# Causal mask by a matmul behind the scores, score banks in twos, casts moved to POOL, loads with third buffers

## The chip, the cores and the metric

The kernel runs on one core of a Trainium2 chip. The core has five engines that run side by side, each through its own list of instructions in order: TensorE (PE; its weight loads are shown apart as PEld), VectorE (DVE), ScalarE (ACT), GpSimd (POOL) and SyncE (SP), which here only issues transfers. TensorE writes to PSUM, eight banks of 128 partitions x 512 float32 words. The metric is the time of one execution on the device in microseconds (us). TensorE's clock has two levels, 1.2 and 2.4 GHz; the profile gives what was granted as a share of the higher one.

## The reference

Attention over 4 batches x 8 heads, 576 positions, head size 64, then two feed-forward blocks. The change touches attention alone.

```python
def _attn_ref(q, k, v, s):
    scores = scale * np.matmul(q, k.transpose(0, 1, 3, 2))
    causal = np.triu(np.ones((S, S), dtype=bool), k=1)
    cum = np.cumsum(np.maximum(s, 0.0), axis=-1)
    bias = -(cum[:, :, :, None] - cum[:, :, None, :])
    scores = np.where(causal, -1000000000.0, scores + np.minimum(bias, 0.0))
    scores = scores - np.max(scores, axis=-1, keepdims=True)
    attn = np.exp(scores)
    attn = attn / (np.sum(attn, axis=-1, keepdims=True) + 1e-09)
    return np.matmul(attn, v)
# then, on x = attention's output as 2304 rows of 512:
#   h = max(x @ w1, x @ w2, x @ w3);  x2 = h @ w_out
#   each row of x2 goes to one of 8 experts:  gate * (relu(x2 @ w1[e]) @ w2[e])
```

Because the bias of a row is the same but for a constant that the softmax removes, a key's bias alone (a running sum of s, times 8) is added to the scores. Everything above the diagonal must vanish after the exponential.

## The kernel before, in words

**A step is one pair of heads**; there are 16 (PORD gives their order). The two heads' q and k lie in the upper and lower 64 partitions. For precision each of q and k is split (split, L199 to 212) into a rounded part, made by a copy on ScalarE (L208), and the rest, made by a subtraction on POOL (L209), both in the tile hl; a score is the sum of three products of such parts.

**Scores** (L217 to 266). The 576 queries are cut into five chunks (QC), and a chunk sees only the keys up to its own end: 576, 448, 320, 192 and 64 of them. The 576 are done in two halves of 288. A chunk or half is a group of six matmuls of 64 rows (L247), three for each head, the heads in turn, into one bank per head from a pool of three (ps_s). VectorE then does one instruction per head (L253): score plus bias into SBUF (tile e), with the running minimum as a side result, since the sign is turned. ScalarE takes the exponential and its row sum (L261).

**The mask** is part of the bias. POOL adds a triangle of -8e9 to the last 128 columns of the key bias bt before it is used (L232), again for the next chunk once VectorE has used the one before (L257), and into a copy bs for the two smallest chunks (L233, L234).

**Behind the scores** each step's e is transposed on PE, 28 blocks of 128x128 into banks of a pool of three (ps_t, L292), copied out by VectorE and ScalarE in turn (L295, L297), and multiplied by v (L318, L321). The reciprocal of the row sums (L271, L272) goes through PE and a round trip to DRAM to become the factor rb, with which VectorE scales the result (L322). This runs a step or so behind the scores.

**Two side jobs** run in the same time. Weights of the first feed-forward block arrive as 64-bit numbers and are converted (convert, L112 to 129): request on SP, then ScalarE (L119), VectorE (L120 to 122), a DMA from POOL (L124) and POOL (L127). From the sixth step on, PE also does a part of that block's projections in the gaps ("fill", L140 to 144).

**What sets the order.** A scheduler orders each engine's instructions by priorities and by its own model of times when the program is built; issue_after ties one instruction behind another, high_priority draws it forward. The kernel asks for loads two steps ahead (L_AHEAD); whether a load can start is decided by its buffers: two for q and k (QR_BUFS), four of bt, two steps' worth (B_BUFS), two for raw weights (RAW_BUFS). SP issues in order, so that a load that waits for its buffer holds those behind it. After attention come the rest of the first block, the routing and the experts, which the change leaves alone.

## Time and profile before

| | |
|---|---|
| Median of 3 runs | 831.02 us (830.81 to 872.44) |
| The profiled execution | 835.91 us, span 834.1 us |
| Busy share of the span | PE 91%, PEld 77%, DVE 61%, ACT 45%, POOL 51% |
| Mean granted clock of TensorE | 0.956 |
| DMA over the span | 129 GB/s |

The span runs from the first to the last instruction of the profiled execution. Busy shares are means over stages of different kinds: attention ends at about 313 us, and what a change there is worth has to be read from that part. In a row of the trace, "out<-in" names the tiles written and read, and an engine's idle time is put down to what it waited for last.

### The profile page before, as it was taken

What the parts mean: (1) busy time and instruction counts of PE and PEld (TensorE: products, weight loads), DVE (VectorE), ACT (ScalarE), POOL (GpSimd) and SP (SyncE); (2) the same over time, 40 slices, a digit from 0 to 9 for tenths busy, and PEclk for the clock granted to TensorE, in tenths of its full rate; (3) what the DMA queues carried; (4) which work ended last, traced back from release to release, by engine and by line L of the source; (5) the groups of instructions that cost most, each with busy time, mean ns of one, the idle gap of its engine ahead of it and who ended that gap; (6) DMA issues with size and microseconds to landing.
All of it is one profiled execution on the core that took longest, in us unless ns stands there. A gap on an engine that the chain in (4) does not pass through costs nothing.

```text
span 834.1 us, 14064 instructions
## 1 busy us (share of the span) xinstructions
PE 759.9 (91%) x4778; PEld 645.0 (77%) x4778; DVE 511.1 (61%) x1382; ACT 376.9 (45%) x924; POOL 425.2 (51%) x484
## 2 busy tenths in 40 slices
PE   2958899979999999989999999999799799999993
PEld 1635566757777878969999989998688699999882
DVE  6556564656554556878466879466464667667720
ACT  2646555545555544442222232165354555656621
POOL 6566565454534402572324363386345767766730
PEclk9988799969999999999999999999899999999998
DMA  7455644436432114421110211375643757656610
GB/s 203 140 147 161 179 132 122 132 119 189 147 101 95 46 39 163 149 94 44 10 49 11 58 46 27 86 265 168 118 157 139 253 191 254 238 195 237 205 48 17
DMA packets 43265, 107.89 MB, mean 129 GB/s; under 512 B 9200, under 2 KB 13168, under 8 KB 43184
## 3 DMA queue, kind: packets, MB, share of 16 engines
q1 hardware_dynamic: 38128, 94.79, 36.4%
q0 software_dynamic: 4912, 11.82, 4.5%
q8 instruction: 39, 0.64, 0.4%
q14 instruction: 42, 0.34, 0.1%
q10 hardware_dynamic: 144, 0.29, 0.1%
HBM read 92.95 MB, written 12.10 MB: 126 GB/s over the span
## 4 chain that ended last, share of the span: by engine, by line
PE 52%; DMA 16%; DVE 13%; POOL 7%; issue 6%; ACT 2%; SPq 1%; POOLq 0%; DVEq 0%; ACTq 0%
PE a_ps L140 5%; PE t_ps L292 5%; PE a_ps L143 5%; PE a_ps L144 4%; PE s_ps L247 4%; DMA w_raw<-in_w 4%; PE o_ps L318 4%; DMA e_raw<-in_we 3%; PE h_ps L650 3%; PE h_ps L653 3%; PE h_ps L654 3%; PE y_ps L681 3%; PE y_ps L682 3%; DMA table<-meta,si 3%; PE y_ps L683 3%
## 5 line engine op out<-in xcount | busy, mean ns | idle before, releaser
L140 PE MATMUL a_ps<-xh,w_h 128*128 128x384 f32 (+2 forms) x492 | 161.1, 328 | 1.7 <-DVE h L346 1.3
L143 PE MATMUL a_ps<-xl,w_h 128*128 128x384 f32 (+2 forms) x492 | 158.6, 322 | 0.9 <-POOL xl L335 0.9
L144 PE MATMUL a_ps<-xh,w_l 128*128 128x384 f32 (+2 forms) x492 | 157.2, 320 | 0.8 <-POOL w_l L127 0.8
L620 DVE TENSOR_TENSOR e_l<-e_raw,e_h 128x512 fp32r<-128x512 f32 x80 | 111.1, 1402 | 52.5 <-ACT e_h L619 50.6
L620 POOL TENSOR_TENSOR e_l<-e_raw,e_h 128x512 fp32r<-128x512 f32 x80 | 108.9, 1382 | 39.4 <-ACT e_h L619 32.4
L247 PE MATMUL s_ps<-hl 64*128 64x288 f32 (+4 forms) x576 | 86.6, 367 | 34.6 <-DVE mn L253 27.9
L619 ACT CAST e_h<-e_raw 128x512 fp32r<-128x512 f32 x160 | 93.1, 621 | 54.9 <-DMA e_raw<-in_we 45.8
L261 ACT ACTIVATE e<-e,mn 128x576 f32<-128x576 f32 (+2 forms) x144 | 83.6, 582 | 51.4 <-DVE mn L253 51.2
L247 PEld LDWEIGHTS s_ps<-hl 64*128 64x128 f32 x576 | 54.1, 208 | 58.6 <-DVE mn L253 36.7
L140 PEld LDWEIGHTS a_ps<-xh,w_h 128*128 128x128 f32 x492 | 93.2, 190 | 6.0 <-DVE h L346 3.0
L143 PEld LDWEIGHTS a_ps<-xl,w_h 128*128 128x128 f32 x492 | 93.2, 189 | 3.7 <-POOL xl L335 1.4
L144 PEld LDWEIGHTS a_ps<-xh,w_l 128*128 128x128 f32 x492 | 93.1, 189 | 1.5 <-POOL w_l L127 1.0
L507 DVE CUSTOM_DVE_ANT_0 junk<-x,wg 128x512 bf16<-128x512 f32 x96 | 71.4, 743 | 27.9 <-ACT x L581 26.7
L650 PE MATMUL h_ps<-x2t,e_h 128*128 128x256 f32 x288 | 80.5, 284 | 4.4 <-DVE gl L656 4.2
L653 PE MATMUL h_ps<-x2t,e_h 128*128 128x256 f32 x288 | 81.5, 284 | 0.0
L654 PE MATMUL h_ps<-x2t,e_l 128*128 128x256 f32 x288 | 81.3, 283 | 0.0
L568 POOL TENSOR_TENSOR fl<-h,fh 128x384 fp32r<-128x384 f32 x36 | 43.8, 1220 | 71.9 <-ACT fh L567 64.0
L292 PE MATMUL t_ps<-ident,e 128*128 128x128 f32 x448 | 70.8, 303 | 1.2 <-ACT r_t L276 0.8
L681 PE MATMUL y_ps<-e_h,gh 128*128 128x512 f32 x152 | 62.6, 412 | 5.8 <-ACT gh L655 5.4
L292 PEld LDWEIGHTS t_ps<-ident,e 128*128 128x128 f32 x448 | 56.5, 155 | 11.7 <-issue 4.4
L253 DVE CUSTOM_DVE_ANT_0 e<-s_ps,bt 128x288 f32<-128x288 f32 (+2 forms) x96 | 47.1, 519 | 23.5 <-POOL bt L257 12.2
L683 PE MATMUL y_ps<-e_h,gl 128*128 128x512 f32 x152 | 61.3, 403 | 0.0
(180 smaller groups left out, 1535.7 us busy)
## 6 DMA issues: line engine op xcount, KB each, us to landing
e_raw<-in_we SPq DMA_DIRECT2D x80, 512.0 KB
w_raw<-in_w SPq DMA_DIRECT2D x24, 512.0 KB
qk_r<-in_qk SPq DMA_DIRECT2D x15, 576.0 KB
bt<-dk SPq DMA_DIRECT2D x30, 288.0 KB
v_r<-in_vd SPq DMA_DIRECT2D x16, 320.0 KB
rb<-r_d SPq DMA_DIRECT2D x32, 144.0 KB
x2d<-x SPq DMA_DIRECT2D x18, 256.0 KB
w_h<-w_z POOLq DMA_DIRECT2D x9, 256.0 KB, 4.9
```

Source lines behind the costliest of these rows:

```text
L140: ins = P.matmul(a_ps, wh[:, c], xh[:, c], start=c == 0, stop=False).ins
L143: P.matmul(a_ps, wh[:, c], xl[:, c], start=False, stop=False)
L144: P.matmul(a_ps, wl[:, c], xh[:, c], start=False, stop=c == 3)
L247: ins = P.matmul(s_ps[j], flat[js, o:o + 128], hl[js, b, 0, k0:k0 + n], start=i == 0, stop=i == 2).ins
L292: last_t[0] = P.transpose(out=t_ps[:, n * 128:(n + 1) * 128], in_=e[:, EOFF[c] + kb * 128:EOFF[c] + (kb + 1) * 128], identity=ident).ins
L619: A.copy(out=h, in_=raw[:, a])
L620: (G if a else V).tensor_tensor(out=lo, in0=raw[:, a], in1=h.bitcast(F32), op=ALU.subtract)
L650: ins = P.matmul(h_ps, w(hs, f, c), xt[:, 0, c], start=c == 0, stop=False).ins
L653: P.matmul(h_ps, w(hs, f, c), xt[:, 1, c], start=False, stop=False)
L654: P.matmul(h_ps, w(ls, f, c), xt[:, 0, c], start=False, stop=c == 3)
L681: P.matmul(y_ps, u["h"][:, f, cs], hs[f], start=f == 0, stop=False)
L683: P.matmul(y_ps, u["l"][:, f, cs], hs[f], start=False, stop=f == NF2 - 1)
```

## The change

1. **Mask on PE.** Behind the six matmuls of a chunk, two bf16 matmuls (one per head) add the product of a diagonal of -2^33 (neg) and a triangle of ones (tri; tri_2 for the smallest chunk) to the last 128 columns of the scores; VectorE's -0.125 turns that into a large positive number. All additions on POOL go, and bs with them.
2. **Score banks in twos.** ps_s has two buffers of two banks (both heads in one tile) in place of three of one bank; ps_t has two banks in place of three.
3. **Casts on POOL.** The rounded parts of q and k are made by POOL, but for the first step.
4. **Third buffers** for q and k and, by the pair, for the bias.
5. **Raw weights a step ahead.** Their request is issued in the step before the one that converts them.
6. At the start, the identity and the constants come over ScalarE's queue, and VectorE does one of the first step's subtractions.

```diff
@@ -72,6 +72,6 @@
 FILL_N = [0, 9, 8, 6]
-PSB = (3, 3, 1, 1)
+PSB = (2, 2, 1, 1)
 HL_BUFS = 2
-QR_BUFS = 2
-B_BUFS = 4
+QR_BUFS = 3
+B_BUFS = 6
 E_N = 4
@@ -111,5 +111,9 @@
 
-        def convert(f, k, pool, tag, rp_, lo_on=None, early=False):
+        def raw_in(f, k, rp_):
             raw = rp_.tile([128, 512, 2], I32, tag="raw", name="w_raw")
             SP.dma_start(out=raw.rearrange("p n c -> p (n c)"), in_=w64[f, :, k * 512:(k + 1) * 512].bitcast(I32))
+            return raw
+
+        def convert(f, k, pool, tag, rp_, lo_on=None, early=False, raw=None):
+            raw = raw_in(f, k, rp_) if raw is None else raw
             h = pool.tile([128, 512], F32R, tag=tag, name="w_h")
@@ -160,3 +164,5 @@
             ps_f = es.enter_context(tc.tile_pool(name="ps_f", bufs=PSB[3], space=PSUM))
-            mask = ap1.tile([128, 256], F32, name="mask")
+            cst_f = ap1.tile([128, 192], F32, name="cst_f")
+            neg = ap1.tile([128, 128], BF16, name="neg")
+            tri_2 = ap1.tile([128, 64], BF16, name="tri_2")
             xb = [None] * B
@@ -188,4 +194,4 @@
                 if p == 0:
-                    SP.dma_start(out=mask, in_=cst[:, 256:512])
-                    SP.dma_start(out=ident, in_=cst[:, 0:128])
+                    A.dma_start(out=ident, in_=cst[:, 0:128])
+                    A.dma_start(out=cst_f, in_=cst[:, 128:320])
                 return p, x, bts
@@ -201,12 +207,13 @@
                 hl = qkp.tile([128, 2, 2, S], F32R, name="hl", bufs=HL_BUFS)
+                for t in (1, 0):
+                    (G.tensor_copy if p else A.copy)(out=hl[:, 0, t], in_=x[:, t])
                 if p == 0:
-                    for t in (1, 0):
-                        A.copy(out=hl[:, 0, t], in_=x[:, t])
-                    decay(bts[0], cums[:, 0])
+                    G.tensor_scalar(out=neg, in0=ident, scalar1=-2.0 ** 33, scalar2=None, op0=ALU.mult)
+                    G.tensor_copy(out=tri, in_=cst_f[:, 0:128])
+                    G.tensor_copy(out=tri_2, in_=cst_f[:, 128:192])
                 for t in (1, 0):
-                    if p:
-                        A.copy(out=hl[:, 0, t], in_=x[:, t])
-                    ins = G.tensor_tensor(out=hl[:, 1, t], in0=x[:, t], in1=hl.bitcast(F32)[:, 0, t], op=ALU.subtract).ins
+                    ins = (V if p == 0 and t else G).tensor_tensor(out=hl[:, 1, t], in0=x[:, t], in1=hl.bitcast(F32)[:, 0, t], op=ALU.subtract).ins
                 if p == 0:
-                    decay(bts[1], cums[:, 1])
+                    for j in range(2):
+                        decay(bts[j], cums[:, j])
                 return ins, (hl, bts)
@@ -227,10 +234,2 @@
                 sums.append(l)
-                bss = []
-                for j in range(2):
-                    bt = bts[j]
-                    bs = qkp.tile([128, 256], F32, name="bs", bufs=B_BUFS)
-                    G.tensor_tensor(out=bt[:, 448:576], in0=bt[:, 448:576], in1=mask[:, 128:256], op=ALU.add)
-                    G.tensor_tensor(out=bs[:, 64:256], in0=bt[:, 0:192], in1=mask[:, 64:256], op=ALU.add)
-                    G.tensor_tensor(out=bs[:, 0:64], in0=bt[:, 0:64], in1=mask[:, 0:64], op=ALU.add)
-                    bss.append(bs)
                 for c in (4, 3, 2, 1, 0):
@@ -239,3 +238,4 @@
                     for k0, n in [(0, w)] if c < 4 else [(0, 288), (288, 288)]:
-                        s_ps = [ps_s.tile([128, 512], F32, name="s_ps")[:, 0:n] for _ in range(2)]
+                        s_2 = ps_s.tile([128, 2, 512], F32, name="s_ps")
+                        s_ps = [s_2[:, j, 0:n] for j in range(2)]
                         ins = None
@@ -246,3 +246,6 @@
                                 with tc.high_priority() if ins else ExitStack(), tc.issue_after(ins) if ins else ExitStack():
-                                    ins = P.matmul(s_ps[j], flat[js, o:o + 128], hl[js, b, 0, k0:k0 + n], start=i == 0, stop=i == 2).ins
+                                    ins = P.matmul(s_ps[j], flat[js, o:o + 128], hl[js, b, 0, k0:k0 + n], start=i == 0, stop=i == 2 and k0 + n < w).ins
+                        for j in range(2 if k0 + n == w else 0):
+                            with tc.high_priority(), tc.issue_after(ins):
+                                ins = P.matmul(s_ps[j][:, max(n - 128, 0):n], neg, tri_2 if c == 0 and j else tri[:, 0:min(n, 128)], start=False, stop=True).ins
                         for j in range(2):
@@ -251,8 +254,4 @@
                             ec = es_[j][:, EOFF[c] + k0:EOFF[c] + k0 + n] if c else e0[rows]
-                            bias_ = bts[j][:, k0:k0 + n] if c > 1 else bss[j][:, 64:256] if c else bss[j][rows, 0:64]
-                            V.tensor_tensor_reduce(out=ec, in0=s_ps[j][rows], in1=bias_, scale=-0.125, scalar=first[j], op0=ALU.add, op1=ALU.min, accum_out=mn[rows, col:col + 1])
+                            V.tensor_tensor_reduce(out=ec, in0=s_ps[j][rows], in1=bts[j][rows, k0:k0 + n], scale=-0.125, scalar=first[j], op0=ALU.add, op1=ALU.min, accum_out=mn[rows, col:col + 1])
                             first[j] = mn[rows, col:col + 1]
-                            if c > 2 and k0 + n == w:
-                                k1 = QC[c - 1][1] - 128
-                                G.tensor_tensor(out=bts[j][:, k1:k1 + 128], in0=bts[j][:, k1:k1 + 128], in1=mask[:, 128:256], op=ALU.add)
                     for j in range(2 if c else 1):
@@ -424,2 +420,3 @@
             todo = []
+            raws = {}
             n_head = 2
@@ -440,4 +437,7 @@
                 for n in CONV.get(p, ()):
-                    with tc.issue_after(exps[-1 - CONV_LAG]), tc.issue_after(last_load[0]):
-                        convert(n // 3, n % 3, w0p, "w0", rawp, early=True)
+                    with tc.issue_after(exps[-1 - CONV_LAG]):
+                        convert(n // 3, n % 3, w0p, "w0", rawp, early=True, raw=raws.pop(n))
+                for n in CONV.get(p + 1, ()):
+                    with tc.issue_after(last_load[0]):
+                        raws[n] = raw_in(n // 3, n % 3, rawp)
                 if p % (H // 2) == H // 2 - 1:
...
```

The parts left out move the constants' columns in the table cst and their loads after the first step.

The order of PE in the fourth step, before (s_ps are scores, t_ps transposes and r the row sums):

```order
L247 MATMUL s_ps<-hl 128x288 x12
L247 MATMUL s_ps<-hl 128x448 x6
L247 MATMUL s_ps<-hl 128x320
L274 MATMUL t_ps<-ident,r 9x128
L292 MATMUL t_ps<-ident,e_119 128x128 x8
L247 MATMUL s_ps<-hl 128x320 x5
L292 MATMUL t_ps<-ident,e_119 128x128 x2
L247 MATMUL s_ps<-hl 128x192
L292 MATMUL t_ps<-ident,e_119 128x128 x4
L292 MATMUL t_ps<-ident,e_120 128x128 x4
L247 MATMUL s_ps<-hl 128x192 x5
```

and now, in the same step, from its chunk of 448 on:

```order
L247 MATMUL s_ps<-hl 128x448 x6
L250 LDWEIGHTS neg
L250 MATMUL s_ps<-tri,neg 128x128
L250 LDWEIGHTS neg
L250 MATMUL s_ps<-tri,neg 128x128
L320 MATMUL t_ps<-pt,v_r 64x64 x2
L273 MATMUL t_ps<-ident,r 9x128
L247 MATMUL s_ps<-hl 128x320 x6
```

Before, one matmul of a chunk stood apart from the other five, with transposes between; now the six stand together and two mask matmuls behind them, and the transposes come between whole groups.

The order of POOL about the first conversions of weights, before (hl is the split q and k, bt and bs the bias, w_h and w_l converted weights):

```order
L209 TENSOR_TENSOR hl<-qk_r,hl 128x576 x2
L124 DMA w_h<-w_z 128x512
L257 TENSOR_TENSOR bt<-bt,mask 128x128 x4
L127 TENSOR_TENSOR w_l<-w_z,w_h 128x512
L124 DMA w_h<-w_z 128x512
L232 TENSOR_TENSOR bt<-bt,mask 128x128
L127 TENSOR_TENSOR w_l<-w_z,w_h 128x512
L232 TENSOR_TENSOR bt<-bt,mask 128x128
L233 TENSOR_TENSOR bs<-bt,mask 128x192
L234 TENSOR_TENSOR bs<-bt,mask 128x64
```

and now, at the same place:

```order
L209 CAST hl<-qk_r 128x576 x2
L215 TENSOR_TENSOR hl<-qk_r,hl 128x576
L128 DMA w_h<-w_z 128x512
L215 TENSOR_TENSOR hl<-qk_r,hl 128x576
L131 TENSOR_TENSOR w_l<-w_z,w_h 128x512
```

Before, mask additions stood behind weight instructions that wait for a DMA; now casts and subtractions of q and k stand there.

The order of SP about the first raw weights, before (r_d and rb are the sums' round trip):

```order
L277 DMA r_d<-r_t 2x1x64
L279 DMA r_d<-r_t 4x128 x2
L179 DMA qk_r<-in_qk 128x1152
L282 DMA rb<-r_d 64x576 x2
L186 DMA bt<-dk 128x576 x2
L114 DMA w_raw<-in_w 128x1024 x2
L216 DMA v_r<-in_vd 128x640
```

and now:

```order
L185 DMA qk_r<-in_qk 128x1152
L192 DMA bt<-dk 128x576 x2
L114 DMA w_raw<-in_w 128x1024 x2
L276 DMA r_d<-r_t 2x1x64
L278 DMA r_d<-r_t 4x128 x2
L281 DMA rb<-r_d 64x576 x2
```

Before, the raw weights stood behind the second step's round trip; now they stand ahead of the first step's. Each request still stands behind two loads of the bias.

## Rows read from the trace of the kernel before

**Rows 1.** Windows: stretch, length, busy time (count) of PE, PEld, DVE, ACT, POOL; clock, DMA.

```profile
24.30:52.40 28.10, 26.27 (x183) 17.65 (x184) 15.36 (x63) 18.03 (x56) 14.06 (x24) 1.00 0.45 127
52.40:95.70 43.30, 30.69 (x181) 19.77 (x179) 24.22 (x79) 21.24 (x60) 25.20 (x37) 0.73 0.54 168
95.70:172.30 76.60, 71.04 (x511) 53.01 (x509) 45.66 (x144) 41.54 (x119) 41.12 (x60) 0.95 0.45 138
172.30:196.70 24.40, 19.85 (x115) 14.16 (x115) 13.18 (x37) 10.25 (x31) 11.92 (x18) 0.72 0.44 136
196.70:219.60 22.90, 21.52 (x168) 17.23 (x166) 16.71 (x49) 12.39 (x34) 11.26 (x17) 1.00 0.56 166
219.60:312.40 92.80, 92.74 (x715) 73.36 (x714) 48.22 (x173) 48.56 (x145) 37.69 (x60) 1.00 0.25 78
```

**Rows 2.** Timeline of the fourth step: start, duration, engine and instruction, [idle before <-releaser].

```profile
49.35 0.90 SPq L114 DMA_DIRECT2D w_raw<-in_w  x2
...
56.25 0.66 ACT L119 ACTIVATE w_z<-w_raw 128x512 f32<-128x512 f32 x1 [5.01 <-DMA w_raw<-in_w]
...
56.94 0.55 DVE L120 TENSOR_SCALAR w_z<-w_z 128x512 int32<-128x512 int32 x1 [3.46 <-ACT w_z L119]
...
58.77 1.22 PE L247 MATMUL s_ps<-hl 64*128 64x288 f32 x6 [4.83 <-DVE mn L253]
```

**Rows 3.** Timeline of the fifth step.

```profile
75.89 0.45 DVE L120 TENSOR_SCALAR w_z<-w_z 128x512 int32<-128x512 int32 x1 [3.02 <-ACT w_z L119]
...
79.36 1.48 PE L247 MATMUL s_ps<-hl 64*128 64x448 f32 x5 [2.65 <-DVE mn L253]
...
87.08 1.27 POOL L127 TENSOR_TENSOR w_l<-w_z,w_h 128x512 fp32r<-128x512 f32 x1 [4.75 <-DMA w_h<-w_z]
...
88.80 0.49 DVE L253 CUSTOM_DVE_ANT_0 e<-s_ps,bt 128x320 f32<-128x320 f32 x1 [1.85 <-POOL bt L257]
...
89.35 1.13 PE L247 MATMUL s_ps<-hl 64*128 64x64 f32 x6 [1.63 <-DVE mn L253]
```

**Rows 4.** Timeline of the tenth step.

```profile
175.39 3.39 DVE L271 TENSOR_SCALAR r<-l 128x9 f32<-128x9 f32 x1
...
176.01 2.74 POOL L209 TENSOR_TENSOR hl<-qk_r,hl 128x576 fp32r<-128x576 f32 x2
...
179.09 0.38 PE L274 MATMUL t_ps<-ident,r 128*9 128x128 f32 x1 [2.71 <-DVE r L272]
```

**Rows 5.** Waits of 24.3 to 219.6 us: who for whom, us, times, longest.

```profile
DVE e L253 <- POOL bt L257: 9.7, 6, 3.1
...
PE s_ps L247 <- DVE mn L253: 18.2, 13, 4.8
...
ACT w_z L119 <- DMA w_raw<-in_w: 16.9, 8, 5.0
```

**Rows 6.** Timeline of PE in the thirteenth step.

```profile
243.70 0.87 PE L247 MATMUL s_ps<-hl 64*128 64x448 f32 x6
244.50 1.31 PE L292 MATMUL t_ps<-ident,e 128*128 128x128 f32 x10
245.57 0.38 PE L140 MATMUL a_ps<-xh,w_h 128*128 128x288 f32 x1
...
252.57 0.29 PE L247 MATMUL s_ps<-hl 64*128 64x64 f32 x1
252.79 0.40 PE L144 MATMUL a_ps<-xh,w_l 128*128 128x288 f32 x1
```

**Rows 7.** Groups of POOL by form: busy us, mean ns, idle before.

```profile
L209 POOL TENSOR_TENSOR hl<-qk_r,hl 128x576 fp32r<-128x576 f32 x32 | 47.2, 1495 | 2.4 <-ACT hl L204 2.0 <-ACT hl L208 0.3
...
L397 POOL CAST tri<-tri_f 128x128 bf16<-128x128 f32 x1 | 0.3, 287 | 0.0
```

**Rows 8.** Groups of DVE, then one line's instructions with min/median/max ns.

```profile
L271 DVE TENSOR_SCALAR r<-l 128x9 f32<-128x9 f32 x16 | 8.9, 557 | 9.8 <-ACT e L261 9.8
...
L271 DVE TENSOR_SCALAR r<-l x16: 163/175/3390, 26.6 to 313.4; 128x9 f32<-128x9 f32 x16
```

More of the change, by code (lines that the diff above doesn't have):

```diff
@@ L392, in fused_kernel @@
             queue(0, front(0), vv)
-            tri_f = ap1.tile([128, 128], F32, name="tri_f")
-            SP.dma_start(out=tri_f, in_=cst[:, 128:256])
-            G.tensor_copy(out=tri, in_=tri_f)
             G.memset(ones, 1.0)
             G.memset(acc[:, 0, :], 0.0)
-            SP.dma_start(out=off, in_=cst[:, 512:512 + E])
-            SP.dma_start(out=iota, in_=cst[:, 520:584])
+            SP.dma_start(out=off, in_=cst[:, 320:320 + E])
+            SP.dma_start(out=iota, in_=cst[:, 328:392])
             sent = ap1.tile([128, TABLE // 128, 2], F32, name="sent")
@@ L886, in _layout @@
     e2 = i["moe2_w2"].reshape(E, 4, 2, 128, DM).transpose(0, 1, 3, 2, 4).reshape(E, 4, 128, 1024)
-    cst = np.zeros((128, 584), np.float32)
+    cst = np.zeros((128, 392), np.float32)
     cst[:, 0:128] = np.eye(128)
     cst[:, 128:256] = np.triu(np.ones((128, 128)), 1)
-    cst[:, 384:512] = np.triu(np.full((128, 128), -8.0e9), 1)
-    cst[:, 256:320] = np.tile(cst[0:64, 384:448], (2, 1))
-    cst[:, 512:520] = np.arange(E) * STRIDE
-    cst[:, 520:584] = np.arange(64)
+    cst[:, 256:320] = np.tile(np.triu(np.ones((64, 64)), 1), (2, 1))
+    cst[:, 320:328] = np.arange(E) * STRIDE
+    cst[:, 328:392] = np.arange(64)
     csi = (np.arange(NT)[None, :] * 128 + np.arange(128)[:, None]).astype(np.int32)
```

## The prediction, made before the changed kernel was run

> **What bounds the kernel now.** I read the table of windows first, then the timeline inside the worst windows, then the waits, and last the pitch of TensorE's instructions.
>
> The windows [rows 1] cut attention at the starts of its 16 steps (a step is one pair of heads). From 24.30 us (second step) to 312.40 us it takes 288.1 us. In the last 92.80 us of that PE is busy 92.74 us at clock 1.00: it is the bound there, and nothing that another engine saves shows. Before that it loses time in two ways: it idles, and after idling its granted clock falls to the lower level, 1.2 GHz, so that its work takes twice as long. A window's idle time is its length less PE's busy time; its loss to the clock is its length times (1 - PEclk). In the order of the rows: 1.8 + 0; 12.6 + 11.7; 5.6 + 3.8; 4.6 + 6.8; 1.4 + 0; 0.1 + 0. That is 26.0 idle and 22.3 by the clock, 48.3 us in all, and half of it, 24.3 us, lies in the fourth and fifth steps, 52.40 to 95.70. The last 520 us, after attention, are touched by no part of the change.
>
> Why PE idles there is seen in the timelines. In the fourth step [rows 2] the raw weights are asked for at 49.35 and are used by ScalarE only at 56.25, after 5.01 us of waiting; VectorE stands behind that with its in-order conversion (3.46 us), and the matmul of the scores behind VectorE (4.83 us). In the fifth [rows 3] there are two spells: PE waits 2.65 us for VectorE, which did late raw weights first (3.02 us of waiting for them), and then a mask addition comes late from POOL, in whose order (w_h, w_l) instructions that wait for a DMA stand ahead of it: VectorE waits 1.85 us for the masked bias, and PE 1.63 us for VectorE. In the tenth step [rows 4] the small TENSOR_SCALAR of the row sums takes 3.39 us while POOL works through two subtractions, and PE waits 2.71 us for it. The waits of 24.3 to 219.6 us [rows 5] give the sums: VectorE waits 9.7 us for the masked bias, ScalarE 16.9 us for raw weights, PE 18.2 us for VectorE's reductions of the scores.
>
> **The change, part by part.** The sum is made against the profiled execution, 835.9 us; it stands 4.9 us (0.6%) over the median of the runs, 831.0, and the result is shifted by that.
>
> *Waits that lose their cause.* With third buffers the bias for the step after next no longer waits for this step's scores; raw weights are asked for a step ahead of their conversion, and a step is some 14 us where it is short (two take 28.10 us [rows 1]) against the 6.9 us from request to use in [rows 2]; and VectorE needs nothing of POOL any more for its bias. So the causes in the fourth and fifth steps go. I take 20 of the 24.3 us in 52.40 to 95.70, 7 of 11.4 in 172.30 to 196.70 (what held VectorE there were mask additions and two subtractions of POOL; the subtractions stay), 6 of 9.4 in 95.70 to 172.30 and 1 of the remaining 3.3: **-34 us**. Ends: nothing (each wait replaced by the next late thing) and -48. Next late is VectorE itself, with 24.22 us of work in the 43.30 us of two steps [rows 1].
>
> *The mask matmuls.* 5 chunks x 2 heads x 16 steps = 160, 128 columns wide on a full 128x128 weight (32 of them 64 wide). No bf16 matmul of that width is in the trace. The nearest row is the transpose, also 128 columns on 128x128: ten take 244.50 to 245.57, 0.107 us each [rows 6]. 160 x 0.107 = **+17 us**, on the path wherever PE is the bound. Ends: 0 (hidden in PE's idle time) and 0.22 each, which is what a single matmul takes until one of another kind starts (252.57 to 252.79), +35; I keep to the transposes, since two masks stand together and transposes or their like follow.
>
> *Score groups that are no longer cut.* By the order of instructions, PE issued the first matmul of a group of six ahead and the other five after other work, because a third single bank was free. With banks in twos the six stand together. Such a lone matmul costs 0.22 us before the next can start [rows 6] (252.57 to 252.79); by streams alone it would be hidden in its pair. A late step has five of them, but a row [rows 6] shows that a lone one which joins the five of the group before costs little (six in 0.80 us, 243.70 to 244.50), so I count three: 15 x 3 x 0.22 = **-10 us**. Ends: 0 and -16 (all five).
>
> *Later hand-over.* VectorE may read a chunk only after the two mask matmuls: 0.21 us, which counts where PE in turn waits for VectorE, 13 times [rows 5]: **+3 us**. Ends 0 and +17, for all 80 chunks.
>
> *POOL.* All 160 mask additions go, and 30 casts come. A cast of 128 columns took 287 ns, the two-input subtraction of 576 columns 1495 ns [rows 7]; these are the ends for a cast of 576, and I take their middle, 0.9 us. So 27 us come (9 to 45). A step's splitting, 2 x 0.9 + 2 x 1.5 = 4.8 us, has a step to run in, and its input is buffered three deep: nothing on the path. What remains is that it holds VectorE, as in [rows 4]: the TENSOR_SCALAR of the sums has a median of 175 ns and a mean of 557 [rows 8], so 16 x 0.38 = 6 us were lost to it, and for the casts I add two thirds of that: **+4 us**, ends 0 and +41 (the last rival). Beside this stands a rule. The Trainium skill, "SBUF — State Buffer", section "Who interferes with whom", says that VectorE's copies, casts and tensor_scalars can take a port pair that it shares with GpSimd, and that whoever comes second is blocked for the whole instruction. That rule speaks against casts on POOL, and if it held every such instruction to the end of the run, the time would be that of the last rival; the trace agrees with the 3.39 us [rows 4], while the median of 175 ns [rows 8] says that most steps escape.
>
> *Two banks for transposes in place of three.* Four transposes fill a bank in 0.43 us (4 x 0.107), and the bank must be copied out before it is filled again. Where PE has no projection to put between them (the first four steps after the first) it may wait for one bank a step, 0.43 us: **+2 us**, ends 0 and +7 (all 16 steps). The casts taken off ScalarE are costed at nothing: it is busy 152.00 of 288.10 us, and what it serves late is its waiting for others. The casts' own lateness on POOL is covered by their lead of a step; without it PE's first matmul of a step would wait the 4.8 us. The new order at the start is costed at nothing either: the same scans of VectorE stand ahead of the first reduction in both.
>
> Sum: -34 + 17 - 10 + 3 + 4 + 2 = -18; 835.9 - 18 = 817.9, and less the 4.9 us **813 us** for the median (-2.2%). A difference of 2%, 16.6 us, is about what a measurement of this kernel tells from none, so the forecast stands on that edge.
>
> **The rivals.**
> 1. *The stall moves* (no change). The five conversions and reductions of a step stay on VectorE in order; when the raw weights come early, VectorE's own queue or the two transpose banks set the step. For it: 24.22 us of VectorE in two steps, with 30.69 of PE at 0.73. Against it: the second and third step, without conversions, ran in 28.10 us for two at full clock. Half of the 34 stays, so -1: 830.
> 2. *All stalls vanish.* PE is then the bound throughout: -48 + 17 - 10, and no late hand-over: -41, 790. For it: the last 92.80 us show that state. Against: the first steps have too little for PE to do.
> 3. *Not a step ahead.* The raw requests stand on SP's queue behind two bias loads that wait for VectorE, so they may go out late; then 12 of the 20 us in steps four and five stay: 825.
> 4. *VectorE held by the casts* (slower). The run of casts and subtractions begins when a step's last score matmul frees the buffer; the TENSOR_SCALAR of that step's sums comes soon after, behind one reduction and one exponential. If VectorE is held to the end of the run in every step, as in [rows 4], PE waits 2.71 us in 15 steps: +41 in place of +4, 850. It decides from the point where the hold is longer than PE's queued transposes (1.07 us for ten). Against it: the median of 175 ns [rows 8].
>
> **How the numbers follow.** Forecast, 804 to 822 with its ends: 0.45. Rival 1 (822 to 834): 0.30. Rival 2: 0.10. Rival 3: 0.06. Rival 4: 0.09. The likeliest is 813. The range that leaves out rival 4 and the half of rival 2 below 793 is 793 to 834. Faster by over 2% is under 814.4: rival 2 and 36 of the forecast's 45 parts at most; I take 0.10 + 0.36 = 0.46. Slower by over 2% is over 847.6: 0.09. The rest is 0.45.
>
> **What would show it.** PE's clock 1.00 or near it from 24 us to the end of attention, and no wait of ScalarE for w_raw there: the first term. The mask's matmul rows with starts 0.1 us apart: the second. Score groups of six with no lone first: the third. CAST rows of 128x576 on POOL near 0.9 us, and the TENSOR_SCALAR of the sums (L270) near 0.17 us: the fourth; several of them over 2 us would be rival 4. PE waiting longer for VectorE's reductions than 18.2 us would be rival 1, and w_raw still awaited rival 3. If the last five steps, where PE was full, took over 95 us, the second and third terms don't cancel as I have it.

## The result, and the profile after

The changed kernel takes 808.7 us (median of 4 runs, 807.3 to 812.3) against 831.0; the ratio is 0.974 (0.970 to 0.978). The profiled execution took 807.35 us, its span is 805.5, the mean granted clock 0.969 (before 0.956). The forecast was 813, the range 793 to 834.

Attention's last matmul into o_ps (the product with v) ends at 302.1 us in place of 322.7: 20.6 of the 28.6 us by which the two profiled executions differ (the medians differ by 22.3). This time is the measure for what follows, because what comes after it is not steady: from there to PE's last instruction it was 491.0 us in this trace, 506.8 in another execution of the same program (e9, below), and 499.1 in the kernel before. The 8.1 us that the two first traces differ by there are no effect of the change that I can show.

The windows, by the starts of the same steps as in [rows 1] (second to third step, fourth and fifth, sixth to ninth, tenth, eleventh, the last five) and, in the last row, from the last score to attention's end; columns as there:

```profile
22.10:44.30 22.20, 20.70 (x159) 14.32 (x157) 14.97 (x62) 14.09 (x46) 8.90 (x10) 1.00 0.68 232
44.30:77.70 33.40, 28.33 (x205) 17.17 (x204) 23.01 (x71) 16.44 (x51) 14.01 (x14) 0.85 0.58 181
77.70:148.70 71.00, 67.00 (x533) 49.83 (x532) 46.69 (x149) 38.14 (x117) 31.99 (x33) 0.95 0.48 156
148.70:165.60 16.90, 15.24 (x127) 11.06 (x126) 10.86 (x38) 9.82 (x30) 10.29 (x11) 1.00 0.53 161
165.60:186.80 21.20, 19.78 (x163) 15.77 (x162) 15.50 (x44) 9.36 (x29) 6.83 (x7) 1.00 0.61 188
186.80:277.70 90.90, 90.72 (x754) 72.71 (x753) 50.45 (x174) 45.59 (x139) 25.38 (x28) 1.00 0.23 74
277.70:302.30 24.60, 20.44 (x140) 15.25 (x138) 18.73 (x43) 12.69 (x28) 7.83 (x6) 0.86 0.36 111
```

Read as before, idle plus loss to the clock: 1.5; 5.1 + 5.0; 4.0 + 3.6; 1.7; 1.4; 0.2. That is 22.4 us over the six windows where [rows 1] had 48.3: 25.9 us less. The fourth and fifth steps give 14.2 of them, the tenth 9.7, the sixth to ninth 1.8. The last window loses 4.2 + 3.4 = 7.6 us; before, the same stretch (10.5 us long, since all projections of this stage were already done, and 36 of them now stand there) lost 3.8.

Now the fourth step, which answers to [rows 2]; timeline: start, duration, engine and instruction, [idle before <-releaser].

```profile
23.32 1.03 SPq L114 DMA_DIRECT2D w_raw<-in_w  x2
...
43.72 1.25 ACT L123 ACTIVATE w_z<-w_raw 128x512 f32<-128x512 f32 x2
...
45.48 1.25 DVE L125 SCALAR_TENSOR_TENSOR w_z<-w_raw,w_z 128x512 int32<-128x512 int32 x1
...
47.66 0.68 DVE L125 SCALAR_TENSOR_TENSOR w_z<-w_raw,w_z 128x512 int32<-128x512 int32 x1
...
48.38 0.62 DVE L294 COPY pt<-t_ps 128x512 f32<-128x512 f32 x1
...
49.06 2.85 PE L291 MATMUL t_ps<-ident,e 128*128 128x128 f32 x10 [1.76 <-DVE pt L294]
```

The raw weights are asked for 20 us before they are used and nobody waits for them. The stall did not vanish, though: the conversions themselves stand in VectorE's order ahead of the copy that frees a transpose bank, and PE waits 1.76 us for that. The sixth step shows the same with POOL in it:

```profile
78.65 3.48 POOL L215 TENSOR_TENSOR hl<-qk_r,hl 128x576 fp32r<-128x576 f32 x2
...
80.79 1.62 DVE L124 TENSOR_SCALAR w_z<-w_z 128x512 int32<-128x512 int32 x1
...
83.51 1.12 PE L291 MATMUL t_ps<-ident,e 128*128 128x128 f32 x4 [1.53 <-DVE pt L294]
...
84.94 2.30 POOL L334 TENSOR_TENSOR xl<-x,xh 128x288 fp32r<-128x288 f32 x3
...
85.29 2.51 DVE L126 SCALAR_TENSOR_TENSOR w_z<-w_raw,w_z 128x512 int32<-128x512 int32 x1
```

A conversion of 0.43 us takes 1.62, one of 0.68 takes 2.51, each while POOL subtracts. The waits of 22.1 to 186.8 us, which answer to [rows 5]:

```profile
DVE e L255 <- PE s_ps L250: 16.3, 22, 1.9
...
PE t_ps L291 <- DVE pt L294: 6.7, 6, 1.8
...
PE t_ps L291 <- ACT pt L296: 2.3, 5, 0.6
...
PE t_ps L298 <- DVE pt L294: 1.5, 3, 1.0
...
DVE w_z L124 <- ACT w_z L123: 1.6, 3, 0.6
...
PE s_ps L247 <- DVE mn L255: 1.5, 3, 0.6
```

PE's wait for the reductions fell from 18.2 to 1.5 us. What is left is 6.7 + 2.3 + 1.5 = 10.5 us for the copies out of the two transpose banks, which is most of the 13.9 us that PE idles in the six windows. In the kernel before, with three banks, such waits came to 0.3 us from 24.3 to 219.6:

```profile
PE t_ps L292 <- DVE pt L295: 0.3, 1, 0.3
```

The mask, in a late step (answers to [rows 6]):

```profile
215.25 0.87 PE L247 MATMUL s_ps<-hl 64*128 64x448 f32 x6
216.05 0.28 PE L250 MATMUL s_ps<-tri,neg 128*128 128x128 bf16 x2
216.26 2.81 PE L317 MATMUL o_ps<-pt,v_r 128*64 128x512 f32 x20
...
220.33 0.58 PE L247 MATMUL s_ps<-hl 64*128 64x192 f32 x6
220.84 0.28 PE L250 MATMUL s_ps<-tri,neg 128*128 128x128 bf16 x2
220.94 0.38 PE L144 MATMUL a_ps<-xh,w_h 128*128 128x288 f32 x1
```

Two masks take 0.21 us (216.05 to 216.26) or 0.10 (220.84 to 220.94), by what follows. On POOL and VectorE ([rows 7, 8]): groups by form, then one line's min/median/max ns.

```profile
L215 POOL TENSOR_TENSOR hl<-qk_r,hl 128x576 fp32r<-128x576 f32 x31 | 47.2, 1540 | 2.4 <-ACT hl L209 2.2
L209 POOL CAST hl<-qk_r 128x576 fp32r<-128x576 f32 x30 | 22.8, 789 | 79.3 <-PE s_ps L247 78.1 <-DMA qk_r<-in_qk 1.2
```
```profile
L270 DVE TENSOR_SCALAR r<-l x16: 153/175/1394, 23.2 to 279.5; 128x9 f32<-128x9 f32 x16
```

The table of all kernels. "End" is the end of attention's last matmul into o_ps (four small ones of 0.3 us together follow); "scores", "mask" and "PE's work" add up, from the second step's first score to that end, the time from each matmul's start to the next one's start or its own end, whichever is earlier, taken at half where the clock was 1.2 GHz (also ahead of the trace's first record of the granted clock, 31.0 us before and 28.2 after: six score matmuls of 448 columns take 1.49 us there in the changed kernel, 0.87 later); "lost" is the rest of the stretch; "lone" counts score matmuls that stand alone. (A window's busy time also holds the modelled ends of matmuls, so its idle time is not quite "lost".) Ratios are to the kernel before on the same chip; they leave out runs that fell into a slower state, which the medians include.

| kernel | median us | ratio | end | PE's work | scores | mask | lost | lone |
|---|---|---|---|---|---|---|---|---|
| before | 831.0 |  | 322.7 | 248.4 | 63.5 | 0 | 50.0 | 20 |
| changed | 808.7 | 0.974 (0.970 to 0.978) | 302.1 | 248.4 | 53.4 | 11.5 | 31.6 | 0 |
| e1 raw weights not ahead | 818.0 | 0.972 (0.964 to 0.979) | 304.2 | 249.0 | 53.4 | 11.4 | 33.0 | 0 |
| e2 two buffers | 820.5 | 0.976 (0.969 to 0.984) | 297.7 | 249.3 | 53.4 | 11.4 | 26.2 | 0 |
| e3 casts on ScalarE | 832.2 | 0.988 (0.981 to 0.995) | 312.7 | 247.5 | 52.6 | 12.2 | 43.7 | 0 |
| e4 three single banks | 840.0 | 0.992 (0.987 to 0.997) | 330.5 | 271.6 | 76.1 | 13.2 | 34.4 | 66 |
| e5 e1 and e2 together | 833.7 | 0.991 (0.986 to 0.996) | 310.6 | 249.7 | 52.2 | 11.2 | 38.7 | 0 |
| e6 no mask | 807.6 | 0.959 (0.949 to 0.969) | 292.8 | 234.6 | 50.3 | 0 | 36.5 | 0 |
| e7 mask on POOL | 825.7 | 0.980 (0.971 to 0.990) | 312.8 | 238.3 | 52.1 | 0 | 49.6 | 0 |
| e8 before, banks in twos | 839.4 | 0.997 (0.992 to 1.001) | 318.8 | 235.3 | 51.2 | 0 | 59.7 | 0 |
| e9 changed, again | 816.8 | 0.967 (0.961 to 0.972) | 301.6 | 248.8 | 53.4 | 11.5 | 30.7 | 0 |
| e10 one pair spread | 818.8 | 0.972 (0.969 to 0.974) | 304.2 | 249.0 | 53.0 | 11.8 | 32.9 | 0 |
| e11 both pairs moved | 815.7 | 0.968 (0.962 to 0.973) | 305.0 | 248.5 | 52.7 | 11.8 | 34.3 | 0 |
| e12 four single banks | 836.1 | 0.993 (0.988 to 0.999) | 312.6 | 260.0 | 62.2 | 11.0 | 31.3 | 31 |

The experiments ran on three chips (e1 to e4 and e9 to e11 on one, e5 to e8 on one, e12 on one), where the kernel before took 842 to 844 us and not 831, so a median is compared within its chip only, and across chips by its ratio. The end of attention and the ratio need not agree: e4 ends attention 7.8 us later than the kernel before and yet takes 0.8% less. What follows attention differs by as much between executions (491.0 and 506.8), and its part in each ratio is left open.

### The profile page after: what moved, and what is told of

It reads as the page before. It is cut to its first block, busy times and chain, and to the rows that moved or that the text cites. A ratio compares the mean times of both kernels' runs of the same rounds, so it can differ in the third digit from the quotient of the medians.

```text
span 805.5 us, 14177 instructions
## 1 busy us (share of the span) xinstructions
PE 750.6 (93%) x4938; PEld 640.4 (80%) x4938; DVE 509.6 (63%) x1383; ACT 358.5 (45%) x894; POOL 375.0 (47%) x355
## 5 line engine op out<-in xcount | busy, mean ns | idle before, releaser
L147 PE MATMUL a_ps<-xl,w_h 128*128 128x384 f32 (+2 forms) x492 | 156.7, 319 | 0.0
L260 ACT ACTIVATE e<-e,mn 128x576 f32<-128x576 f32 (+2 forms) x144 | 83.4, 580 | 74.5 <-DVE mn L255 74.2
L255 DVE CUSTOM_DVE_ANT_0 e<-s_ps,bt 128x288 f32<-128x288 f32 (+4 forms) x160 | 63.9, 426 | 33.2 <-PE s_ps L250 26.8
L247 PE MATMUL s_ps<-hl 64*128 64x288 f32 (+4 forms) x576 | 68.1, 344 | 14.9 <-DVE mn L255 8.7
L291 PE MATMUL t_ps<-ident,e 128*128 128x128 f32 x448 | 69.7, 292 | 12.0 <-DVE pt L294 6.7
L247 PEld LDWEIGHTS s_ps<-hl 64*128 64x128 f32 x576 | 44.8, 198 | 29.8 <-DVE mn L255 9.5
L291 PEld LDWEIGHTS t_ps<-ident,e 128*128 128x128 f32 x448 | 53.1, 149 | 18.8 <-DVE pt L294 9.1
L131 POOL TENSOR_TENSOR w_l<-w_z,w_h 128x512 fp32r<-128x512 f32 x24 | 32.2, 1345 | 71.2 <-ACT w_h L130 45.2
```

The costliest lines, as they stand in the source:

```text
L147: P.matmul(a_ps, wh[:, c], xl[:, c], start=False, stop=False)
L247: ins = P.matmul(s_ps[j], flat[js, o:o + 128], hl[js, b, 0, k0:k0 + n], start=i == 0, stop=i == 2 and k0 + n < w).ins
L260: ex = A.activation(out=ec, in_=ec, func=ACTF.Exp, bias=mn[:, col:col + 1], scale=-1.0, accum_out=l[:, col:col + 1]).ins
L291: last_t[0] = P.transpose(out=t_ps[:, n * 128:(n + 1) * 128], in_=e[:, EOFF[c] + kb * 128:EOFF[c] + (kb + 1) * 128], identity=ident).ins
```

## The experiments

All but e8 start from the changed kernel.

**e9. The changed kernel again** (no edit).

> The changed kernel once more, so that it stands beside the experiments on their chip. If the time after attention is a matter of the chip and not of the edits, it takes about 500 us from the last matmul of attention to PE's last here too, as in six of the experiments, in place of 491 in its first profile, and attention ends at 302 us again; ratio to before 0.970 to 0.978. Otherwise (the edits moved what follows) 491 again.

Attention ended at 301.6 us with every step's start within 1.0 us of the first trace: attention's times can be compared across executions, as far as two traces show it. The rest took 506.8 us in a profiled execution of 822.5, the slowest of four; the median was 816.8. The ratio, 0.967, is a little better than the 0.970 to 0.978 expected, with an interval that overlaps it.

**e1 and e2. Each part of the early loads undone alone; e5, both.**

```diff
 # e1
-                    with tc.issue_after(exps[-1 - CONV_LAG]):
-                        convert(..., raw=raws.pop(n))
-                for n in CONV.get(p + 1, ()):
-                    with tc.issue_after(last_load[0]):
-                        raws[n] = raw_in(n // 3, n % 3, rawp)
+                    with tc.issue_after(exps[-1 - CONV_LAG]), tc.issue_after(last_load[0]):
+                        convert(...)
 # e2
-QR_BUFS = 3
-B_BUFS = 6
+QR_BUFS = 2
+B_BUFS = 4
```

> The changed kernel, but each raw weight is asked for in the step that converts it, as before. My theory (waits that lost their cause): ScalarE waits again for the raw weights, more than 10 us in the steps with a conversion, PE idles behind VectorE and its clock falls there; 8 to 14 us slower than the changed kernel (about 819). Rival (the third buffers alone let the requests go out in time): no wait of ScalarE worth 3 us, time within 3 us of the changed kernel.

> The changed kernel, but with two buffers for q and k and two pairs of bias tiles, as before. My theory: the bias for the step after next waits again for VectorE's last reduction, holds SP's queue and with it the raw weights, which now stand a step ahead and so can bear a delay; 2 to 6 us slower than the changed kernel. Rival (the buffers are what lifted the stall): 10 us or more slower, with ScalarE waiting for raw weights or PE for hl. Second rival (nothing waits on these buffers any more): within 2 us.

> The changed kernel with both undone: raw weights asked for in their own step, and two buffers for q and k and two pairs of bias tiles. Attention's last matmul ended at 302.1 us in the changed kernel, at 304.2 and 297.7 with one of the two undone, at 322.7 in the kernel before. Theory A (each of the two parts alone does for the other, together they carry my first term): attention ends at 312 or later, ScalarE waits more than 8 us for raw weights before 220 us, 10 us or more slower than the changed kernel. Theory B (the late weights were never the cause, or they came late only because VectorE stood behind POOL's mask): attention ends within 4 us of 302, ScalarE waits under 3 us for raw weights.

In the steps neither part alone matters: e1's rival and e2's second rival held there, and the steps of e1 and e2 start within 0.14 us of each other, all sixteen. (By the medians on that chip, 816.8 for e9, 818.0 for e1 and 820.5 for e2, e2's first theory, 2 to 6 us slower, is not excluded; e2's executions spread from 815.3 to 824.1.) Up to the end of the last score these kernels do the same matmuls, and it is reached at 277.7 us in the changed kernel, 278.1 in e1, 278.0 in e2 and 290.9 in e5: the pair is worth 13.2 us there. From there to the end of attention the kernels with third buffers take 24.4 (changed) and 26.1 us (e1), those with two 19.7 (e2 and e5): there the changed kernel has conversions of later weights on ScalarE ahead of a copy that PE waits for, shown with the end below; e2's order has them later. So at the end of attention 8.5 us are left of the pair's 13.2, and e2 ends 4.4 us before the changed kernel. The timeline of e5, to be set against 23.32 and 43.72 above:

```profile
46.77 1.84 SPq L114 DMA_DIRECT2D w_raw<-in_w  x2
...
52.58 0.66 ACT L123 ACTIVATE w_z<-w_raw 128x512 f32<-128x512 f32 x1 [3.28 <-DMA w_raw<-in_w]
53.27 0.43 DVE L124 TENSOR_SCALAR w_z<-w_z 128x512 int32<-128x512 int32 x1 [3.16 <-ACT w_z L123]
...
53.77 2.81 PE L317 MATMUL o_ps<-pt,v_r 128*64 128x512 f32 x20 [2.21 <-ACT pt L296]
```

and the waits of e5 from 22 to 220 us:

```profile
ACT w_z L123 <- DMA w_raw<-in_w: 20.5, 7, 5.1
DVE w_z L124 <- ACT w_z L123: 20.2, 7, 4.1
```

The same request in e1 and, second, in e2:

```profile
32.27 0.90 SPq L114 DMA_DIRECT2D w_raw<-in_w  x2
...
32.18 0.90 SPq L114 DMA_DIRECT2D w_raw<-in_w  x2
```

It goes out at 46.8 us with neither part, at 32.3 with the third buffers alone, at 32.2 with the step ahead alone, at 23.3 with both; the weights are wanted at about 44. Either part moves it by a step, and one step is enough: ScalarE has no wait for raw weights from 22 to 220 us in e1 and e2. Theory A's chain holds; attention's end, 310.6, is short of the 312 that it named.

**e3. The casts back on ScalarE.**

```diff
-                    (G.tensor_copy if p else A.copy)(out=hl[:, 0, t], in_=x[:, t])
+                    A.copy(out=hl[:, 0, t], in_=x[:, t])
```

> The changed kernel, but all casts of q and k stand on ScalarE, as before. My theory (ScalarE had time, the casts on POOL hold VectorE for about 4 us): between 4 us faster and 2 us slower than the changed kernel, with PE's order of work much the same in kind. Rival (the casts were late on ScalarE, behind its exponentials, and POOL's subtractions behind them): 6 us or more slower, with PE waiting for hl at the starts of steps.

10.6 us more, 8.6 of them in the second to sixth steps (83.1 in place of 74.5 us). The loss is the rival's in size but not in kind: PE does not wait for hl. The second step of e3, timeline:

```profile
21.88 1.23 ACT L209 CAST hl<-qk_r 128x576 fp32r<-128x576 f32 x2
...
23.01 0.34 ACT L260 ACTIVATE e<-e,mn 128x64 f32<-128x64 f32 x1
...
23.48 0.57 DVE L270 TENSOR_SCALAR r<-l 128x9 f32<-128x9 f32 x1 [1.42 <-ACT e L260]
24.08 0.46 DVE L255 CUSTOM_DVE_ANT_0 e<-s_ps,bt 128x288 f32<-128x288 f32 x1
...
24.98 1.49 PE L247 MATMUL s_ps<-hl 64*128 64x448 f32 x6 [1.35 <-DVE mn L255]
...
40.31 0.87 PE L247 MATMUL s_ps<-hl 64*128 64x448 f32 x6 [0.56 <-DVE mn L255]
```

The two casts stand in ScalarE's order ahead of the step's last exponential. VectorE waits 1.42 us for its row sum (L270), the next step's reduction stands behind that, and PE behind the reduction, 1.35 us. Then the same six matmuls take 1.49 us, and 0.87 a step later: PE stayed at the lower level of its clock until 37.8 us (the first record of 2.4 GHz), in the changed kernel, which has no such wait there, until 28.2. That is some 10 us more at half speed, about half of the 10.6; "lost" rises by 12.1, PE's work not at all. The rest was not followed row by row; from 22 to 220 us PE's wait for VectorE's copies of the transposes (L291 for L294) is 11.2 us, where the changed kernel has 6.7.

**e4 and e12. Single score banks: three (and three transpose banks), and four (and two).**

```diff
-PSB = (2, 2, 1, 1)
+PSB = (3, 3, 1, 1)      # e12: (4, 2, 1, 1)
-                        s_2 = ps_s.tile([128, 2, 512], F32, name="s_ps")
-                        s_ps = [s_2[:, j, 0:n] for j in range(2)]
+                        s_ps = [ps_s.tile([128, 512], F32, name="s_ps")[:, 0:n] for _ in range(2)]
```

> The changed kernel, but with three single score banks and three transpose banks, as before (mask on PE kept). My theory: lone score matmuls come back, three a step that cost 0.22 us each, 10 us slower, less about 2 us of transpose waits saved: 8 us slower than the changed kernel. Rival (the lone matmul is hidden in its pair, and a third bank lets PE run ahead of VectorE): within 2 us or faster.

> The changed kernel with its four score banks as four single buffers, one head each, in place of two of two; the two transpose banks stay. The experiment with three single banks had 66 lone score matmuls, and PE's time for scores rose from 55.2 to 78.3 us. Theory A (a lone matmul goes ahead because one bank is free while the other is not, whatever their number): 20 or more lone matmuls, attention ends at 308 or later. Theory B (the odd number of banks was the cause; with four, both heads' banks come free together): fewer than 8 lone matmuls, attention ends within 3 us of 302.

The groups are cut again, 66 times and 31 times, and PE's work rises by 23.2 and 11.6 us. e12's theory A holds: not the number of banks but the tile that holds both heads keeps the six together. What one cut costs is seen in e4's PE timeline:

```profile
222.62 0.47 PE L246 MATMUL s_ps<-hl 64*128 64x448 f32 x1
223.02 1.31 PE L290 MATMUL t_ps<-ident,e 128*128 128x128 f32 x10
...
225.84 0.87 PE L246 MATMUL s_ps<-hl 64*128 64x448 f32 x5
226.65 0.28 PE L249 MATMUL s_ps<-tri,neg 128*128 128x128 bf16 x2
```

The lone matmul takes 0.40 us and the other five still 0.81, as long as six together (215.25 to 216.05, above). So a cut costs the whole lone matmul: 0.22 us for 64 columns, 0.28 for 192, 0.34 for 320, 0.40 for 448 (means of e4 at the higher clock). That is 0.18 us more for 384 columns more; most of the 0.22 at 64 is not a matter of columns, and no run here tells what it is. The Trainium skill, "TensorEngine Tiling (Array Packing)", section "Key Properties", says that different tiles can load weights and multiply in parallel; the trace agrees: of the five that are left three belong to one head, and they take as long as six.

**e6. The mask matmuls left out** (the mask is not applied at all).

```diff
-                        for j in range(2 if k0 + n == w else 0):
-                            ...
-                                ins = P.matmul(s_ps[j][:, max(n - 128, 0):n], neg, ..., start=False, stop=True).ins
```

> The changed kernel without the mask: the two matmuls behind each chunk are left out, so that keys above the diagonal take part; all other work is the same. The trace of the changed kernel gives 11.7 us of PE's time to 150 of them (78 ns each until the next matmul starts). My theory, by the pitch of the transposes and the later hand-over: 17 + 3, so attention ends near 282. Rival (the second weight load and stream are hidden): 11.7 us by the rows, at most 13, attention ends near 290. Second rival (PE idles elsewhere instead): under 5 us.

9.3 us less: the rival by the rows held. PE's work falls by 13.8 us, 11.5 of them the mask's own (11.7 before the first microseconds are taken at half) and 3.1 the scores' beside them (50.3 against 53.4), and 4.9 come back as lost time (36.5 against 31.6).

**e7. The mask back on POOL** (q and k with two buffers, three pairs of bias tiles).

```diff
+                    G.tensor_tensor(out=bt[:, 448:576], in0=bt[:, 448:576], in1=mask[:, 128:256], op=ALU.add)
+                    ...
-                                ins = P.matmul(s_ps[j][:, max(n - 128, 0):n], neg, ..., start=False, stop=True).ins
```

> The changed kernel with the mask back on POOL as additions to the bias; score banks in twos, casts on POOL, raw weights a step ahead and three pairs of bias tiles stay, q and k have two buffers for lack of room. PE loses 12 us of mask matmuls. Theory A (POOL's additions were the root of the waits): VectorE waits for masked bias again for 10 us or more, attention ends at 308 or later. Theory B (the banks in twos are what the change is worth, the mask's place is neutral or worse on PE): attention ends at 290 to 298, faster than the changed kernel.

10.7 us later in attention although PE has 10.1 us less to do: 18 us more are lost, and the second step begins 2.8 us later. (That q and k have two buffers is not it: e2, with two, loses nothing in the steps.) The waits of 22 to 220 us say that it is not by way of the masked bias:

```profile
PE s_ps L253 <- DVE mn L259: 22.5, 14, 3.9
...
DVE e L259 <- POOL bt L263: 2.1, 1, 2.1
```

So theory A had the time but not the chain. What holds VectorE before those reductions was not taken apart; its instructions run 30.1 us over the shortest of their form in all, 23.5 in the changed kernel.

**e8. The kernel before with the banks in twos alone.**

```diff
-PSB = (3, 3, 1, 1)
+PSB = (2, 2, 1, 1)
-                        s_ps = [ps_s.tile([128, 512], F32, name="s_ps")[:, 0:n] for _ in range(2)]
+                        s_2 = ps_s.tile([128, 2, 512], F32, name="s_ps")
+                        s_ps = [s_2[:, j, 0:n] for j in range(2)]
```

> The kernel before with one thing changed: two score buffers of two banks (both heads in one tile) and two transpose banks in place of three and three. By my third and sixth terms: score groups of six, 10 us less of PE, 2 us more for transposes, all waits for raw weights and masked bias still there: 8 us faster than before, attention ends near 315. Rival (the waits sat behind the cut groups): 15 us or more faster, attention ends near 305. Second rival (the waits take what the groups give): within 3 us of before.

PE's work falls by 13.1 us, lost time takes 9.7 of them back; the time is the same within the measurement. The second rival holds. The waits of 22 to 220 us show where:

```profile
PE t_ps L293 <- DVE pt L296: 9.2, 10, 3.0
PE s_ps L248 <- DVE mn L254: 9.0, 8, 4.3
```

PE's wait for the reductions is half of the 18.2 us before, and in its place PE waits for copies out of the two transpose banks: 9.2 us for VectorE's and 6.2 for ScalarE's.

**e10 and e11. Conversions spread** (beside the table, a conversion in the second step asks for its own weights).

```diff
-CONV = {2: [0, 1], 3: [2], 4: [3, 4], 5: [5], 7: [6], 8: [7], 9: [8]}
+CONV = {1: [0], 2: [1], 3: [2], 4: [3, 4], 5: [5], 7: [6], 8: [7], 9: [8]}      # e10
+CONV = {1: [0, 1], 2: [2], 3: [3], 4: [4], 5: [5], 7: [6], 8: [7], 9: [8]}      # e11
```

> The changed kernel with the two conversions of the third step spread: the first of them is done in the second step; the pair of the fifth step stays. What the changed kernel still loses in 44.3 to 77.7 us (5.1 us idle and 5.0 by the clock) stands behind VectorE's two conversions in its order. Theory A (two conversions at once are the cause): 4 to 8 of these go, attention ends at 294 to 298. Theory B (one conversion is enough to hold the transposes' two banks, or the second step now loses as much): within 2 us of 302.

> The changed kernel with the conversions of the third and fifth steps spread so that the only pair is done in the second step, where PE idles 1.5 us at full clock. Theory A: of the 10.1 us lost in 44.3 to 77.7 and 7.4 in 77.7 to 148.7 us, 8 to 13 go, attention ends at 289 to 294. Theory B: a pair in the second step holds the third as it held the fourth; within 3 us of 302.

Theory B both times: attention ends 2 to 3 us later (e10 0.2 us outside the 2 that it named), no gain. Up to the last score they need 276.8 and 278.5 us, the changed kernel 277.7 (276.7 in e9). In e11 the third step is 19.8 us long in place of 13.0; the stall goes where the pair goes. No version that computes the whole was measured faster than the changed kernel; e2 ends attention earlier, but its ratio does not show it.

## Why the prediction was right, and where its steps were not

**Waits (-34, and +3 +4 +2 against it).** Together these foresaw 25 us less lost; the six windows have 25.9 less. So the net is right; the terms in it are not. The weights' part is shown, but as one cause with two remedies (e1, e2, e5): they are not two gains, and they hold 13.2 us up to the last score, 8.5 at attention's end. The two transpose banks (+2, at most +7) are the term that was most mis-sized: PE waits 10.5 us for the copies that free one, where it waited 0.3 before, and its clock falls again behind such waits (0.85 in the fourth and fifth steps). By runs: with two transpose banks these waits are there in e8, which changes nothing but the two pools of banks (15.4 us), and beside single score banks in e12 (12.5 us from the second step to the tenth); with three of them (e4) PE, which has some 23 us more to do in that kernel, has none in the same steps. No run has three of them beside whole groups: two score buffers of two banks, two for transposes and two others are all eight. Apart from these waits PE idles 3.4 us in the six windows, where it idled 26.0: the old causes went further than the -34 allows for, and the transposes took back more than the sum foresaw. That the two meet near 25 is luck. Rival 1, which named VectorE's queue and these two banks, was half right: in the fourth and fifth steps 10.1 us stay (VectorE's own conversions stand ahead of such a copy, 1.76 us of PE in the rows above), so 14 of the 20 us came. In the sixth to ninth steps 1.8 came for 6, in the tenth 9.7 for 7.

**The mask (+17).** Mis-sized: 11.5 us on PE for 150 matmuls, 77 ns each and not the transposes' 107; 13.8 with what the scores beside them lengthen, and 9.3 on the path (e6). The later hand-over (+3) was not seen: e6 gives back less than the matmuls themselves.

**Groups no longer cut (-10).** The total is right, 10.1 us, its working wrong on both sides: not 45 lone matmuls at 0.22 us but 20, each at 0.22 to 0.40. 20 x 0.3 is 6; the other 4 us of scores I can't lay to single rows. Nor the 3.8 of projections (77.8 to 74.0), and these need not be the groups': e12, with 31 cuts and two transpose banks, has 74.9 us of them, e4, with three, 77.9. Taken alone (e8) banks in twos are worth 4 us of attention, transpose waits included, and without them (e4) the change ends attention at 330.5, later than the kernel before, with 66 groups cut in place of 20. So the term pays in full only where the waits are gone; that the mask pays only where the groups are whole is likely from e4, but no run puts the mask back on POOL beside single banks.

**POOL's casts (+4) and ScalarE's relief (0).** Here the working failed. The casts take 0.79 us (0.9 taken), VectorE's holding is as before (L270 up to 1.39 us in place of 3.39, its conversions up to 2.51): over the shortest of each form some 24 us in all, some 21 to 22 before, so 2 to 3 us more, by how the forms are grouped, of VectorE's time and not of PE's. The row of 2.51 us agrees with the Trainium skill, "SBUF — State Buffer", section "Who interferes with whom", for an instruction with two inputs from SBUF beside one of GpSimd's that reads SBUF. Rival 4 is excluded. But the relief that was costed at nothing is worth 10.6 us (e3): I looked at ScalarE's busy share (152 of 288 us) and not at what stands behind the casts in its order.

**The start (0).** The second step begins at 22.1 us, 2.2 earlier than in [rows 1]; it was costed at nothing. The new order of the start alone is not the reason: e4 (single score banks) and e7 (mask on POOL) keep that order and begin at 24.5 and 24.9 us, e8 (banks in twos alone) at 23.8. With the mask on PE and four score banks it begins at 21.3 (e12, single) to 22.3; more was not taken apart.

**The end.** After the last score 3.8 us more are lost than before, a place that the prediction did not look at. The changed kernel's timeline there:

```profile
289.80 0.66 ACT L123 ACTIVATE w_z<-w_raw 128x512 f32<-128x512 f32 x1 [1.03 <-DMA w_raw<-in_w]
290.36 0.24 ACT L275 COPY r_t<-t_ps 9x128 f32<-9x128 f32 x1
...
290.65 2.11 PE L291 MATMUL t_ps<-ident,e 128*128 128x128 f32 x10 [1.67 <-ACT r_t L275]
```

A raw weight of the next stage is late, ScalarE waits for it in order, and the copy that frees one of two transpose banks stands behind. The third buffers bring this about: with two (e2) this stretch is 4.7 us shorter.

**The sum.** By the table the 20.6 us are 18.4 less lost, no change in PE's work and 2.2 from the start. (The windows give 22.1 for the lost time of the same stretch, which is 52.1 less 30.0; the difference is the modelled ends and the clock ahead of its first record.) Foreseen were 25 less lost and 7 more work. So the sum was near because misses cancel, which is luck: the waits gave some 3 to 7 us less than taken, the end included, and the work came out even, the mask (11.5) and transposes (2.1) against scores (10.1) and projections (3.8). The last five steps took 90.9 us, under the 95 that were named as the limit, also with the 12 projections (252 in place of 264, 1.8 us) that now stand behind them.

## What to carry to other kernels

Undo each part of a change alone and then the suspects together: two remedies of one wait each look worthless alone (2 us and nothing) and are worth 8.5 us as a pair (13.2 up to the last score). An engine with half its time free can still be the one to relieve: look at which instruction a move puts at the head of its queue, and who waits for that. When one wait is removed, look at the smallest pool that the change leaves: here a bank taken from the transposes, costed at 2 us, became PE's longest wait. When halves of a packed pair come from separate buffers, a scheduler may start one alone (31 and 66 times here); in one tile they stayed together.

## What had not been expected of the hardware

Five packed score matmuls take as long as six (0.81 and 0.80 us for 448 columns). The time after attention differs by 16 us (491.0 and 506.8) between two executions of one program, the second among the experiments, while attention itself repeats to 0.5 us. And the clock column of a window reads 1.00 where the trace has no record yet: the first row of [rows 1], 24.30 to 52.40, hides 6.7 us at the lower level, 3.4 us of loss that the prediction did not count.
